# New token layout, order table and engine choices in a two-layer linear-attention and top-2 kernel

## Chip, cores and metric

One core of a Trainium2 chip. The metric is the device time of one execution in microseconds (us). The kernel before takes 153.89 us, the median of 3 runs (153.22 to 154.31).

## What is computed

Two equal layers on x of 2048 tokens by 512, in bfloat16. Each layer is an attention block without a softmax, and then a block that changes two rows only:

```python
q, k, v = layernorm(x) @ wqkv            # 32 heads of 16
phi = lambda t: where(t > 0, t + 1, exp(t)) + 1e-6
kv  = sum over tokens of phi(k)^T v      # per head, no mask
z   = sum over tokens of phi(k)
x   = x + ((phi(q) @ kv) / (phi(q) @ z + 1e-6)) @ wo

h   = layernorm(x)
r   = h @ w_r                            # one number per token
idx = the two tokens with the largest r
y   = (silu(h[idx] @ w_gate) * (h[idx] @ w_up)) @ w_down * sigmoid(r[idx])
x   = x + (h, with y added to rows idx)
```

`w_gate` and `w_up` are 512 by 1376, `w_down` 1376 by 512.

## The kernel before

The 2048 tokens are 16 tiles of 128; tile t holds tokens 128t to 128t+127, one per partition. x (16 tiles by 512 columns), its transpose and all weights stay in SBUF. Loads are cut into blocks of 1, 1, 2, 2, 2, 4 and 4 tiles, and the host arrays A_x and A_xt are laid out block by block so that each partition reads one run.

The kernel is a list of 959 small operations (a layer's products, activations, copies, small statistics). Each names its engine or leaves the choice between VectorE (DVE), ScalarE (ACT) and GpSimd (POOL) open. Two strings settle what is issued when, and where. ORDER (L30 on) names the operations one by one, two characters each, and each engine executes its own in that order; a queue never overtakes. PICK (L64 on) holds one letter for each of the 179 operations with a choice: D, A or P. `Plan.table` (L156) walks through ORDER. Semaphores are set from what each operation reads and writes. PSUM holds 3 slots `mm`, 4 `g` and 1 `tp`, which are reused in ORDER's sequence.

What follows is layer 1 in the order of a reader:

- **Ramp.** TensorE spins on zeros (L862) until the first half of wk lands. Tile 0's raw keys are built from wk and x transposed (L420) and a correction (L426) by wl, the column means of wk, which ScalarE copies from PSUM (L879). VectorE makes wkc, the centred wk, by four additions (L881), and the other tiles' raw keys come from wkc (L420). VectorE's statistics are L338 and L340; the factor 1/sigma is ln and exp on ScalarE (L353, L356), with nb behind it (L361).
- **phi.** For raw keys: e and rl on ScalarE (L393, L394), em on VectorE (L395), and pk = rl + em (L398) on VectorE or POOL. xn, the normalised tile, is L325 (ACT) or L327 (DVE, POOL). G (L438) sums pk^T xn over the tiles; its four matmuls per tile wait for pk and xn.
- **Block mask.** L830 multiplies a head pattern that POOL makes (L773, L775) and leaves a block-diagonal mask, copied at L835 and first read when G becomes KV (L504).
- **Queries.** Q products (L453) and their phi (L375 to L386) fill TensorE; pq is scaled with the denominators at L575, KW = KV times wo is copied from PSUM (L317, L319), and the outputs (L591) are added to x (L596) with sums for the next statistics (L611, L642 to L648).
- **Row choice.** L686 and L689 make keys, one per token, whose low bits hold the token's number (from `rid`, L782). L990 takes each partition's largest, L994 transposes them, L999 takes the candidates. In layer 1 `index(0)` (L1001) turns the two winners into row numbers. In layer 2 the two rows are gathered by matmuls: L1391 broadcasts keys, eqE (L1397) marks candidates, L1451 gathers, WL (L1486), L1497 and L1505 pick, xs (L1514) is the input of gate and up (L1523) and of down (L1564).
- **Last output.** `last_out` normalises a tile of x for the output into pk (L325 or L327), with factors from `last_scales` (L1362 to L1364) and `halves` (L1371, L1372), on any of the three engines. Six stores from SP (L1381) write 4, 4, 2, 2, 2 and 2 tiles; L1581 writes the two chosen rows behind them, with row numbers from L1006 and L1010.

L1435 are matmuls on a zero tile that fill TensorE where it waits.

Of the kernel before, what the change touches and what calls it, by code (L numbers as in the profile page):

```python
# [10 lines left out]
I32 = mybir.dt.int32  # L11
U16 = mybir.dt.uint16
ACT = mybir.ActivationFunctionType
ALU = mybir.AluOpType
# [1645 lines left out]
```

## Time and profile before

| what | us |
|---|---|
| median of 3 runs | 153.89 |
| lowest and highest | 153.22, 154.31 |
| the profiled execution | 154.49 |
| its span, first to last instruction | 152.8 |
| mean granted clock of TensorE | 0.971 |

The rows below come from that one execution. In the profile PE is TensorE, PEld its weight load, DVE VectorE, ACT ScalarE, POOL GpSimd, SP SyncE, and a letter q behind them means the engine's sequencer. Times on the timeline are from the start of the span. A row of the timeline with x4 puts four instructions together, from the first one's start to the last one's end. In brackets stands how long the engine was idle before and what ended that. The granted clock is 1.00 when TensorE may run at its full 2.4 GHz, and 0.5 at 1.2 GHz. Matmuls are pipelined, so one of 0.38 us is followed by the next after 0.215.

### The profile page before, as it was taken

The numbers are of one execution on the slowest core, as the hardware profiler recorded it, in microseconds if no ns is written. First come the engines' busy times: TensorE is split into PE (matmuls) and PEld (weight loads), VectorE is DVE, ScalarE is ACT, GpSimd is POOL, SyncE is SP. The second block draws the span as 40 slices with busy tenths as digits, with TensorE's granted clock in tenths as the row PEclk, the third lists the DMA queues.
The fourth block names the chain that finished last, engine by engine and source line by source line (L and its number), as shares of the span: only waits on it lengthen the run. The fifth ranks groups of instructions, "written<-read, shape, count | busy, mean of one in ns | idle before, by whom it ended". The sixth has DMA issues, their size and how long they took to land.

```text
span 152.8 us, 3668 instructions
## 1 busy us (share of the span) xinstructions
PE 144.9 (95%) x1244; PEld 72.0 (47%) x1262; DVE 125.7 (82%) x456; ACT 111.7 (73%) x270; POOL 43.5 (28%) x101
## 2 busy tenths in 40 slices
PE   7999999999999999999999999999999999995990
PEld 2344444454445544444444454546564445562480
DVE  0599999758889999999999586668889999999550
ACT  3299998697287694998988564335498989999730
POOL 7631522350105433405400003110115056460300
PEclk9999999999999999999999999999999999999685
DMA  5999999569980000489644400000000000004660
GB/s 122 375 356 395 245 312 217 81 122 348 198 330 4 0 4 0 102 180 389 121 75 100 96 12 0 6 0 0 4 0 4 0 0 4 2 0 139 210 206 5
DMA packets 23187, 18.20 MB, mean 119 GB/s; under 512 B 18048, under 2 KB 20608, under 8 KB 22784
## 3 DMA queue, kind: packets, MB, share of 16 engines
q1 hardware_dynamic: 22872, 17.57, 42.8%
q10 hardware_dynamic: 296, 0.39, 0.7%
q8 instruction: 10, 0.16, 0.4%
q14 instruction: 9, 0.07, 0.2%
HBM read 11.67 MB, written 2.10 MB: 90 GB/s over the span
## 4 chain that ended last, share of the span: by engine, by line
PE 79%; DVE 13%; DMA 3%; ACT 2%; issue 1%; DVEq 0%; ACTq 0%
PE g L438 18%; PE mm L453 16%; PE mm L420 9%; PE g L591 9%; PE mm L406 9%; DVE x L596 6%; DMA wk<-in_A_wk_dram 3%; DVE pq L575 2%; PE tp L551 1%; PE g L1435 1%; PE g L492 1%; PE g L1523 1%; PE g L1451 1%; PE mm L1078 1%; PE g L534 1%
## 5 line engine op out<-in xcount | busy, mean ns | idle before, releaser
L375 ACT ACTIVATE e<-mm 128x512 bf16<-128x512 f32 x48 | 28.1, 598 | 10.1 <-PE mm L406 5.6
L453 PE MATMUL mm<-xnT,wq 128*128 128x512 bf16 x119 | 31.2, 380 | 0.5
L438 PE MATMUL g<-pk,xn 128*128 128x512 bf16 x126 | 31.4, 379 | 0.1
L591 PE MATMUL g<-KW,pq 128*128 128x512 bf16 (+2 forms) x128 | 29.8, 373 | 0.2
L611 ACT ACTIVATE sq<-x 128x512 bf16<-128x512 bf16 (+2 forms) x31 | 18.8, 608 | 2.0 <-DVE x L596 1.6
L438 PEld LDWEIGHTS <-xn 128*128 128x128 bf16 x128 | 12.1, 98 | 13.8
L591 PEld LDWEIGHTS <-pq 128*128 128x128 bf16 x132 | 12.2, 97 | 13.1
L453 PEld LDWEIGHTS <-wq 128*128 128x128 bf16 x128 | 11.7, 98 | 13.2 <-issue 0.6
L406 PE MATMUL mm<-wk,xnT 128*128 128x512 bf16 x62 | 16.0, 380 | 0.1
L379 DVE TENSOR_SCALAR em<-e 128x512 bf16<-128x512 bf16 x48 | 13.5, 289 | 3.0 <-ACT e L375 2.7
L420 PE MATMUL mm<-wkc,xt 128*128 128x512 bf16 x59 | 14.3, 379 | 0.1
L338 DVE BATCH_NORM_STATS2 st<-x 128x6 f32<-128x512 bf16 x16 | 10.4, 677 | 4.2 <-DMA x<-in_A_x_dram 4.2
L394 ACT ACTIVATE rl<-mm,rho 128x512 bf16<-128x512 f32 x16 | 11.0, 703 | 1.2 <-issue 1.1
L386 DVE SCALAR_TENSOR_TENSOR pk<-mm,em 128x512 bf16<-128x512 f32 x16 | 11.0, 688 | 0.6 <-DVE em L379 0.4
L393 ACT ACTIVATE e<-mm,rho 128x512 bf16<-128x512 f32 x16 | 10.8, 698 | 0.6 <-PE mm L426 0.6
L596 DVE SCALAR_TENSOR_TENSOR x<-x,opr,g 128x512 bf16<-128x512 bf16 (+2 forms) x17 | 11.3, 710 | 0.0
L386 DVE SCALAR_TENSOR_TENSOR pq<-mm,em 128x512 bf16<-128x512 f32 x16 | 10.7, 686 | 0.2
L596 DVE SCALAR_TENSOR_TENSOR x<-x,g 128x512 bf16<-128x512 bf16 x16 | 10.4, 680 | 0.0
L420 PEld LDWEIGHTS <-xt 128*128 128x128 bf16 x64 | 6.2, 98 | 7.8 <-issue 0.5
L378 ACT ACTIVATE rl<-mm 128x512 bf16<-128x512 f32 x16 | 9.4, 595 | 0.5 <-PE mm L453 0.4
L406 PEld LDWEIGHTS <-xnT 128*128 128x128 bf16 x64 | 6.0, 98 | 7.5 <-issue 0.7
L327 POOL TENSOR_SCALAR xn<-x,s,nb 128x512 bf16<-128x512 bf16 x8 | 6.5, 821 | 10.6 <-DVE nb L361 9.9
(297 smaller groups left out, 243.1 us busy)
## 6 DMA issues: line engine op xcount, KB each, us to landing
wgu<-in_B_wgu_dram SPq DMA_DIRECT2D x2, 1408.0 KB, 6.1
wd<-in_B_wd_dram SPq DMA_DIRECT2D x1, 1408.0 KB, 6.9
xt<-in_A_xt_dram SPq DMA_DIRECT2D x2, 512.0 KB, 6.2
x<-in_A_x_dram SPq DMA_DIRECT2D x2, 512.0 KB, 6.9
out_dram<-pk SPq DMA_DIRECT2D x2, 512.0 KB, 3.1
out_dram<-pk SPq DMA_DIRECT2D x4, 256.0 KB, 2.8
xt<-in_A_xt_dram SPq DMA_DIRECT2D x3, 256.0 KB, 4.2
x<-in_A_x_dram SPq DMA_DIRECT2D x3, 256.0 KB, 4.8
```

Of the source, the lines that this page charges most:

```text
L375: act(0.5, lambda: A.activation(out=e()[:], in_=p()[:], func=ACT.Exp), r=[p], w=[e], **k)
L379: dve(0.2, lambda: V.tensor_scalar(out=em()[:], in0=e()[:], scalar1=1.0, scalar2=TINY, op0=ALU.min, op1=ALU.add), r=[e], w=[em], port=True ...
L386: dve(0.6, lambda: V.scalar_tensor_tensor(out=out_ap, in0=p()[:], scalar=0.0, in1=em()[:], op0=ALU.max, op1=ALU.add), r=[p, em], w=[key], **k)
L393: act(0.57, lambda: A.activation(out=e()[:], in_=p()[:], func=ACT.Exp, scale=s_), r=[p, ("rho0", t)], w=[e])
L394: act(0.57, lambda: A.activation(out=rl()[:], in_=p()[:], func=ACT.Relu, scale=s_), r=[p, ("rho0", t)], w=[rl])
L406: T_.matmul(p()[:], lhsT=xnT[:, c, t * P : (t + 1) * P], rhs=wk[:, c, :], start=(c == 0), stop=(c == NC - 1))
L420: T_.matmul(p()[:], lhsT=xt[:, t, c, :], rhs=w_[:, c, :], start=(c == 0), stop=(c == NC - 1 and not raw))
L438: T_.matmul(Gs[c]()[:], lhsT=xn[:, t, gcol(c) : gcol(c) + P], rhs=pk[:, t, :], start=first, stop=last)
L453: T_.matmul(p()[:], lhsT=wq[:, i, c, :], rhs=xnT[:, i, j * D : (j + 1) * D], start=(i == 0), stop=(i == NC - 1))
L591: T_.matmul(p()[:, 0:n], lhsT=pqt(c, t * P, P), rhs=KWs[layer][:, c, a : a + n], start=(c == 0), stop=(c == NC - 1),)
L596: dve(0.07 + 0.6 * n / D, lambda a=a, n=n, p=p, h=h: V.scalar_tensor_tensor(out=x[:, t, a : a + n], in0=x[:, t, a : a + n], scalar=1.0 if ...
L611: A.activation(out=sq()[:, 0:n], in_=xh, func=ACT.Square, scale=float(D) ** -0.5, accum_out=acc)
```

## The change

Three things change.

First, the token layout: token 16p + t now lies in partition p of tile t. The host arrays, the output's pattern, the numbers in `rid` and `index(0)` follow; `index(0)` has two more small instructions on VectorE. A store of four tiles now writes one run of 4 KB per partition.

Second, ORDER is another sequence of the same 959 operations. In most of it the shifts are local; the larger ones are in the first 30 us and from about 110 us on. On SP's queue the loads keep their order at the start, wd stands right behind the second half of wgu, wvn behind all sixteen transposes of layer 2, and the last three stores are of tiles 14 to 16, 12 to 14, and 10 to 12 instead of 10 to 12, 14 to 16 and 12 to 14.

Third, PICK: VectorE has 77 of the choices (79 before), ScalarE 60 (61), POOL 42 (39). In the ramp pk of tile 0 and xn of tiles 1, 3, 4, 6, 7 and 10 go to POOL; pk of tiles 1, 5 and 8 come to VectorE. In the last quarter one pq addition, one KW copy and a few last_out change engines.

```diff
-    out_dram = out.flatten_outer_dims().rearrange("(t p) d -> p t d", p=P)
+    out_dram = out.flatten_outer_dims().rearrange("(p t) d -> p t d", t=NT)
...
-        G_.iota(rid[:], pattern=[[-P, NT]], base=S - 1, channel_multiplier=-1)
+        G_.iota(rid[:], pattern=[[-1, NT]], base=S - 1, channel_multiplier=-NT)
...
         def f():
-            V.tensor_scalar(
-                out=idx[:], in0=g8[:, 0:2].bitcast(I32), scalar1=S - 1, scalar2=S - 1,
-                op0=ALU.bitwise_and, op1=ALU.bitwise_xor,
-            )
+            bits = g8[:, 0:2].bitcast(I32)
+            if i == 0:
+                V.tensor_scalar(
+                    out=lo_[:], in0=bits, scalar1=7, scalar2=(NT - 1) * P, op0=ALU.logical_shift_left, op1=ALU.bitwise_and
+                )
+                V.tensor_scalar(
+                    out=idx[:], in0=bits, scalar1=4, scalar2=P - 1, op0=ALU.logical_shift_right, op1=ALU.bitwise_and
+                )
+                V.scalar_tensor_tensor(
+                    out=idx[:], in0=lo_[:], scalar=S - 1, in1=idx[:], op0=ALU.bitwise_xor, op1=ALU.bitwise_xor
+                )
+            else:
+                V.tensor_scalar(
+                    out=idx[:], in0=bits, scalar1=S - 1, scalar2=S - 1, op0=ALU.bitwise_and, op1=ALU.bitwise_xor
+                )
...
-        "A_x": blocks(inputs["A_x"].reshape(NT, P, D).transpose(1, 0, 2)),
-        "A_xt": blocks(inputs["A_x"].reshape(NT, P, NC, P).transpose(3, 0, 2, 1)),
+        "A_x": blocks(inputs["A_x"].reshape(P, NT, D)),
+        "A_xt": blocks(inputs["A_x"].reshape(P, NT, NC, P).transpose(3, 1, 2, 0)),
...
 ORDER = (
-    "0P8b000Q01030R020e05060708090A0X0B0k3x040Y450S0W0V0Z0f0T0a0g0U0b0r0l463y0y0m0c0h0i0n0w0C170s0o0t0z0D0E0H0F1D0G0x"
+    "0P000Q03010X0Y040R0S0W3y020506070e08090A0B0C0D0f0Z0V0T0E0U0r0a0g0b0c0k0l0H0F0G0d0i0I0w170h0m0n0j1D0y0o0p0s1C0t0z"
```

The first place is TensorE's start, behind the first four raw-key matmuls (L420) of tile 0. E_94 is the head pattern, wl the correction. This is a piece of the difference:

```order
 L420 LDWEIGHTS xt
 L420 MATMUL mm<-wk,xt 128x512
-L830 LDWEIGHTS E_94
-L830 MATMUL mm<-E_94 128x128
 L426 LDWEIGHTS xt
 L426 MATMUL mm<-wl,xt 128x512
```

L830 has left this place; it stands now behind the products that close layer 1's G.

On POOL, from the last of the constants on, before:

```order
L788 MEMSET elast 128x128
L789 AFFINE_SELECT elast<-elast 128x128
L327 TENSOR_SCALAR xn<-x,rho,nb 128x512
L398 TENSOR_TENSOR pk<-rl,em 128x512
L327 TENSOR_SCALAR xn<-x,rho,nb 128x512
L974 MEMSET h_150 128x352
L398 TENSOR_TENSOR pk<-rl,em 128x512 x2
L327 TENSOR_SCALAR xn<-x,rho,nb 128x512
L398 TENSOR_TENSOR pk<-rl,em 128x512
```

and in the changed kernel:

```order
L788 MEMSET elast 128x128
L789 AFFINE_SELECT elast<-elast 128x128
L327 TENSOR_SCALAR xn<-x,rho,nb 128x512
L398 TENSOR_TENSOR pk<-rl,em 128x512
L327 TENSOR_SCALAR xn<-x,rho,nb 128x512 x3
L819 MEMSET KWr 128x128
L819 MEMSET w_73 128x128
L327 TENSOR_SCALAR xn<-x,rho,nb 128x512 x2
L973 MEMSET eqE 128x384
L327 TENSOR_SCALAR xn<-x,rho,nb 128x512 x2
L820 COPY w_73<-wr 128x4
L398 TENSOR_TENSOR pk<-rl,em 128x512
```

The first pk is now tile 0's (before it was tile 1's), the other pk that follows is tile 10's, and seven xn stand between and behind them.

On VectorE around the largest keys (L990), which L994 on TensorE waits for, before:

```order
L648 TENSOR_TENSOR mv<-mv,sums 128x3
L686 SCALAR_TENSOR_TENSOR s_192<-mv,pwr,s_186 128x1
L990 MAX s_190<-keys 128x8
L1362 TENSOR_SCALAR opr<-rho 128x1
L1363 TENSOR_TENSOR rho<-mv,rho 128x1
L1364 TENSOR_TENSOR nb<-rho 128x1
L686 SCALAR_TENSOR_TENSOR s_189<-mv,pwr,s_186 128x3
L689 TENSOR_TENSOR keys<-s_192,rho 128x1
L999 MAX cand<-tp 128x8
L689 TENSOR_TENSOR keys<-s_189,rho 128x3
L1371 CAST sc<-rho 128x3
L1372 TENSOR_TENSOR sc<-rho,sc 128x3
```

and in the changed kernel, whose lines from L1009 on are 11 higher:

```order
L686 SCALAR_TENSOR_TENSOR s_190<-mv,pwr,s_187 128x3
L689 TENSOR_TENSOR keys<-s_189,rho 128x12
L686 SCALAR_TENSOR_TENSOR s_193<-mv,pwr,s_187 128x1
L648 TENSOR_TENSOR mv<-mv,sums 128x3
L990 MAX s_191<-keys 128x8
L327 TENSOR_SCALAR pk<-x,opr,nb 128x512
L1373 TENSOR_SCALAR opr<-rho 128x1
L1374 TENSOR_TENSOR rho<-mv,rho 128x1
L1375 TENSOR_TENSOR nb<-rho 128x1
L689 TENSOR_TENSOR keys<-s_193,rho 128x1
L999 MAX cand<-tp 128x8
L689 TENSOR_TENSOR keys<-s_190,rho 128x3
```

The key term of the last 3 tiles (L686) stands now ahead of L990, and a final normalisation pk, which stood ahead, right behind it. Further on, three pk stand between WL (L1486, now L1497) and xs (L1514, now L1525) on VectorE, where one pair stood behind xs before.

## Rows read from the trace of the kernel before

**Rows 1.** The page's first part: busy time, share of the span, instructions

```profile
PE 144.9 (95%) x1244; PEld 72.0 (47%) x1262; DVE 125.7 (82%) x456; ACT 111.7 (73%) x270; POOL 43.5 (28%) x101
```

**Rows 2.** Waits of PE, whole span: us, times, longest

```profile
PE tp L994 <- DVE rho L1363: 1.6, 1, 1.6
```

**Rows 3.** Busy time by stretches: PE, PEld, DVE, ACT, POOL, PEclk, DMA share, GB/s

```profile
134.00:138.00 4.00, 3.83 (x48) 2.16 (x46) 3.97 (x23) 3.92 (x17) 2.62 (x8) 1.00 0.06 22
138.00:142.00 4.00, 2.43 (x20) 1.26 (x24) 3.58 (x26) 3.92 (x8) 0.60 (x4) 0.83 0.46 155
142.00:146.00 4.00, 4.00 (x83) 2.35 (x76) 2.20 (x10) 3.11 (x4) 0.91 (x2) 0.74 0.59 197
```

**Rows 4.** Timeline 137.5 to 146.5: start, duration, engine, line, operation, idle before

```profile
139.21 0.16 DVE L990 MAX8 s<-keys 128x8 f32<-128x12 f32 x1
...
139.52 0.40 PE L994 MATMUL tp<-identf,s 128*128 128x128 f32 x2 [1.64 <-DVE rho L1363]
...
139.96 0.43 DVE L999 MAX8 cand<-tp 128x8 f32<-128x256 f32 x1
...
140.31 0.15 DVE L689 TENSOR_TENSOR keys<-s,rho 128x3 bf16<-128x3 f32 x1
...
142.75 1.45 PE L1435 MATMUL g<-warm 128*128 128x512 bf16 x3
...
143.21 0.51 DVE L1486 SCALAR_TENSOR_TENSOR WL<-keys,s,sc 128x45 bf16<-128x45 f32 x2
...
144.84 0.17 DVE L1514 TENSOR_REDUCE xs<-tp 128x8 bf16<-128x16 f32 x1 [1.12 <-PE tp L1505]
```

**Rows 5.** The chain that ended last, in time: start, time on the chain, engine, line

```profile
135.89 2.00 DVE x L596 x6
...
140.52 0.82 PE mm L1391 x3
...
145.25 1.78 PE g L1523 x72
...
147.61 1.19 PE g L1564 x44
```

**Rows 6.** Timeline 146.4 to the end, the row number and the row write

```profile
147.75 0.16 DVE L1010 SCALAR_TENSOR_TENSOR s<-s 128x1 int32<-128x1 int32 x1
...
149.57 1.14 ACTq L1581 DMA_DIRECT2D out_dram<-yo  x1
```

**Rows 7.** Timeline of the ramp, 0 to 13.5

```profile
5.38 1.29 DVE L338 BATCH_NORM_STATS2 st<-x 128x6 f32<-128x512 bf16 x2 [4.22 <-DMA x<-in_A_x_dram]
...
5.83 0.60 ACT L879 ACTIVATE wl<-g 128x512 bf16<-128x512 f32 x1 [2.79 <-PE g L876]
...
6.59 0.23 PE L830 MATMUL mm<-E 8*128 8x128 bf16 x1
6.66 1.40 DVE L881 TENSOR_TENSOR wkc<-wk,wl 128x512 bf16<-128x512 bf16 x4
...
6.75 1.04 PE L426 MATMUL mm<-wl,xt 128*128 128x512 bf16 x4
...
7.88 0.69 ACT L393 ACTIVATE e<-mm,rho 128x512 bf16<-128x512 f32 x1 [0.57 <-PE mm L426]
...
10.48 1.03 PE L438 MATMUL g<-pk,xn 128*128 128x512 bf16 x4
```

**Rows 8.** Line 398 (pk): durations in ns min/median/max, first and last start

```profile
L398 DVE TENSOR_TENSOR pk<-rl,em x12: 384/419/426, 9.9 to 35.8; 128x512 bf16<-128x512 bf16 x12
L398 POOL TENSOR_TENSOR pk<-rl,em x4: 1148/1153/1157, 11.0 to 28.1; 128x512 bf16<-128x512 bf16 x4
```

**Rows 9.** DVE's groups by form: count | busy us, mean ns | idle before

```profile
L596 DVE SCALAR_TENSOR_TENSOR x<-x,opr,g 128x512 bf16<-128x512 bf16 x15 | 10.5, 741 | 0.0
...
L327 DVE TENSOR_SCALAR pk<-x,opr,nb 128x512 bf16<-128x512 bf16 x4 | 1.5, 406 | 0.0
...
L686 DVE SCALAR_TENSOR_TENSOR s<-mv,pwr,s 128x3 f32<-128x3 f32 x1 | 0.2, 216 | 0.0
```

More of the change, by code (lines that the diff above doesn't have):

```diff
@@ new lines @@
+    "271r2D1u1g1s0L1S2A1v3z341h1i3E1w1j2R2Z2E2G252Q2F2H2I2J353F2j2u2v26362B1x2C2U2e372w2a202x3j4C1y2K382b8Z2k2L2M2f3G"
+    "4D211z1k3H302c2d2S2T2z393I3J2g3l3k2l2N2h401Q3A2y3U2i312m320M3x2O2n333B3C3D3P2o3Q2p2s4E3m8a3n3S2q2r3Z3b3a3e3K3L3R"
+    "3c3d3T3p3r3q4J4K4L4M442V4F3o3s3N2W2X2t3O4G4H4I3V3u3v3t3w3W4O4N3M3X3Y2Y47485349544A4Q4P4R4S55564r4s8c3f3g454d4e46"
+    "4t4u3h3i4f4T4U4z50514g4h4j4v4w4x524y4k4V4X0N4i4l4m4Z4W4a4b4c5V4Y5W4n4o4q4p5O0O57585X5P5L5S5Q5R595A5B5M5N5T5U5E5F"
+    "5G5D5Z5a5Y5b6P5o6Q5p5c5C5d5q5e5r5s5t5u5H5I5v6B5J6I5K5n5w5x5y626R6y64655f685g6C6D60618X5h66635i6z696A6r6J6X75765j"
@@ new lines @@
+    "6S7C5k8b67706K6E6W5m5l7n8I6Y6T6s6Z6a6b6c7D6d7u6t6F6e6f6U6V777E6g6G6H6h6n6lA3A5A46j8J7oALAM6k7K414BAN7L8P8Q7v7M7N"
+    "6pA9AA6o6L6MABAC7O7P7QAO6N6O7p7J7R7S7T7UAP6u6v81827a6w6x9r7W7wAF7172736m7c839wAD6qAGAH7bA17d84858K74787X79Aj7qAl"
+    "8eAkA27FA87V8R7A8fAI7Y8g868788898AAJ7B7Z8B8C8G8H8EAE427r7s7G7e7H8h8i7I8j7f7g8F8k8l7h8m7i9f9g7t8d8n8o8s8t8q9h7x7y"
+    "8p7z8LAK7j805z6i43AQ7k7l7m8D8r8M8u8N8xAX8v8OAm8w8y8S8T8z9192AYAZ9iAn93949DAWAc96Ad999sAe8U989A8VAiAf9B9C979E9FAo"
+    "9M9G9t9J9u9vAz9NA695909KB09H9IAR9L9P9O9Q9R9jAa9k9l9m9n9o9SA7Ag9UAx9T9p9xAS8WAT9y9q9V9W9XApAqAr9zA09Y9ZAt9a9cB49b"
@@ new lines @@
+    "AUAbB1B28YAVAs9eBLBN9dBMBFBGBHBvAuAvBxBwAhC7BKAwBqBIB8BOBQAyC8CAB9ByC9CBBrBtBsBABPBBBJCTBcBRB3BdBeB6BzBYB5B7BjBk"
+    "BuBUBWBSBCBDBlBZBaBbBfBVBgCZBECbCaBmBnBXCCCECDC0C1BTC2CKCLBhBiCWClCcBoBpCdCMC3C4CFCXCmCnCYCGCHCNCOCICJC5CoCpCqDI"
+    "DJCeCfCgCsCtCuCvC6DFDCDGDKD3DHCrDDCwCyChCiCPCSCQCRDED4CUDMDLCVCkCjD5DND1CxD0DODPDQDVDRDmDnDoDgDjDhDkDXDYDiDlDpEQ"
+    "D6DZD8ERD7D9EUESETEVDqElDAEmDrEnDsDBEDEoEpEECzD2DtDwDxEGEHE4E5DaDbDdDcDeE7EAE8EJEqEKE9EBDfECDuEODvErEWEFEIE6ELEX"
+    "DSEwEYEsEaDTEtEZEMENEPEhEiEjDyEbDUDWEcEdEuExF1EkF2EgEvEeF3DzE2EfEzF0FDFFEyFEE1F4F5F6F7E0E3FGF8FCFHFIF9FAFNFJFKFL"
@@ L49 @@
+    "FOFMFBFQFPFRFS"
 )
@@ L1001, in index @@
     def index(i):
-        idx, pw = small([P, 2], I32), small([P, 1], I32)
+        idx, pw, lo_ = small([P, 2], I32), small([P, 1], I32), small([P, 2], I32)
         g8 = B["g8"]
         def f():
-            V.tensor_scalar(
-                out=idx[:], in0=g8[:, 0:2].bitcast(I32), scalar1=S - 1, scalar2=S - 1,
-                op0=ALU.bitwise_and, op1=ALU.bitwise_xor,
-            )
+            bits = g8[:, 0:2].bitcast(I32)
[13 more added lines that the diff above has]
+                )
             V.scalar_tensor_tensor(
@@ L1012, in f @@
             )
-        dve(0.25, f, r=["g8"], w=["pw"], port=True)
+        dve(0.25 if i else 0.5, f, r=["g8"], w=["pw"], port=True)
         B["idx"], B["pw"] = idx, pw
```

22 lines of the change are left out of this document (3 added, 19 removed).

## The prediction, made before the changed kernel ran

> **What bounds the kernel now.** I began with the shares of the engines: TensorE is busy 144.9 us, 95% of the span, VectorE 125.7 [rows 1]. Next come the waits of TensorE over the whole span: apart from its start there is one, 1.6 us in front of L994, the transposes of the top keys [rows 2]. So up to 137.9 us, where that wait begins (139.52 less 1.64 [rows 4]), nothing that the kernel reorders can be worth more than the little that TensorE loses in steps too short for that list. Third, the stretches of 4 us show who rules the end: VectorE is busy 3.97 us of 4 in 134–138; then TensorE falls to 2.43 us in 138–142, and its granted clock to 0.83 there and 0.74 in 142–146 [rows 3]. With two levels, 1.2 and 2.4 GHz (0.5 and 1), these are 1.4 us of the first and 2.1 us of the second stretch at the lower one, so about 140.6 to 144.1 if they are one piece. The reader is to see three regimes: a ramp in which each TensorE wait counts in full; a long middle with no slack on TensorE; and, from about 117 us, VectorE's queue, which sets when the keys of the last row choice are ready and so when L994 may start. Behind L994 stands a serial tail: L994 139.52, the candidates L999 139.96, the late keys L689 140.31, their broadcasts L1391 140.52, the gather L1451, filling matmuls 142.75, the weights WL 143.21, the sums xs 144.84, gate and up L1523 145.25, down L1564 147.61, and the row writes 149.57 [rows 4 to 6].
>
> The profiled execution is 154.49 us, 0.60 above the median of 153.89; every time below is a difference in that execution, and I carry the sum over to the median unchanged.
>
> **The ramp.** Two things leave the place between the loads and the first G. The block-mask matmul L830 stood between the halves of the first raw-key product: it ran 6.59 to 6.82, and the second half started at 6.75 although its operand wl was done at 6.43 [rows 7]. Behind it, VectorE had two statistics in a row, 5.38 to 6.67, and only then the four additions L881, 6.66 to 8.06, for which the next raw-key products wait [rows 7]. In the new order one statistic stands ahead of the additions and the second behind, so the additions wait for wl: 6.43 plus the step of some 0.1 that other hand-overs take, 6.52. That is 0.14 earlier; the second half may start about 0.16 earlier. I take 0.15. The other end is 0, and the reason is pk(0). Its addition goes from VectorE to POOL, where four additions of that line took 1.153 against 0.419 on VectorE [rows 8]. ScalarE now does e(0) and rl(0) in one row, without the small lnv between them, so with the second half at 6.6 e(0) would start at 7.72 (1.13 behind it, as 7.88 behind 6.75) and both, at 0.69 each, be done at about 9.0 to 9.1; POOL ends at about 10.2, and G(0) wants pk at 10.48 − 0.15 = 10.33 [rows 7]. It fits with a tenth to spare. If it does not, the gain of the ramp is gone first, and what POOL is later than 10.33 is paid one for one.
>
> The trace's ratio of these additions is 2.75. The Trainium skill, in "GPSIMD Engine Reference", § 4.1 Engine selection, sends elementwise work to VectorE and puts two-input operations on GpSimd at about twice as slow. By that ratio the addition would take an estimated 0.84, pk(0) would be ready at 9.9 and no wait would be possible; by the row there is one tenth. The measurement decides.
>
> The xn of tiles 1, 3, 4, 6, 7 and 10 that go to POOL will be slower there too, up to the 0.73 of the addition as a bound, but each is wanted by a G with at least one raw-key product of four matmuls (1.03 [rows 7]) between; pk(1), (5) and (8) come back to VectorE in exchange. I put this at nothing, with those products as cover.
>
> **The layout.** Loads keep their size, their order and one run per partition, because the host array is permuted with them: 0. Stores write one run of 4 KB per partition where they wrote four of 1 KB. The row writes, which wait for all stores, left at 149.57 [rows 6]. But they wait for the row number too: L1010 ends at 147.91 [rows 6], and the registers are loaded behind it. That path is the same in both kernels, so faster stores gain nothing that can be relied on: 0, with 0.2 as the other end. The two additional small instructions of the first row choice (0.16 each, as L1010 [rows 6]) lie beside TensorE's filling work in layer 1: 0. The wvn load moves behind all transposes of the second layer; its first reader, L1239, stands far behind them, where layer 2 turns from keys to outputs: 0.
>
> **VectorE in the last quarter.** Between the first scaling of pq (L575) and the keys' maximum L990 the new order takes out two means (0.16 each, as other small instructions of VectorE [rows 6]) and one final normalisation pk (0.406), and takes in one key term of 3 columns (L686, 0.216) [rows 9]: −0.51 busy. Between KVm (L504) and that first scaling it moves one small instruction (0.16, L677) ahead and puts one pq addition of 0.42 (as L398 [rows 8]) in: +0.26. One KW copy takes the place of another. From KVm on the sum is thus −0.25. A busy microsecond is less than one of the clock, because records overlap: three of the residual additions L596, 0.741 each, and the three short reads of their accumulators (the x6 of the row) carry the chain on by only 2.00, where the additions alone are 2.22 [rows 5, 9]. With the reads I count five sixths. So L990 comes 0.21 to 0.43 earlier, by whether the additional pq addition lies in time that VectorE spent waiting for TensorE's KV products or not. I take 0.30, nearer the low end, since VectorE's queue was already full ahead of the first scaling.
>
> **What is given back behind L990.** The pk that was taken out stands now right behind L990, ahead of the three small scale instructions, the last-but-one key and L999. In before L999 started 0.75 after L990, as soon as L994's result was there (139.52 + 0.40) [rows 4]. Now VectorE has 0.41 more and the 0.22 of L686 less in front of it: L990 + 0.95. The late keys L689 follow L999 by 0.35 as before, and their broadcasts L1391 started 0.2 after 140.31 [rows 4, 5]. So +0.20. The two half-precision instructions that leave the place before eqE make eqE about 0.3 earlier, but L1451 has to wait for L1391 (140.52 + 0.82) anyway: 0.
>
> **The tail.** t15's final normalisation leaves ScalarE, so the table load for the gate starts earlier; but the gate and up products fill TensorE without a break until 147.4 (145.25 + 1.78 and the rest) [rows 5]: 0. Three pk on VectorE now stand between WL (ends 143.72) and xs (144.84) [rows 4]. Three times 0.406 [rows 9] is 1.22 busy, about 1.0 to 1.1 of the clock, in a hole of 1.12: 0, with +0.1 as the near end and one pk, +0.4, as the far end.
>
> **The sum.** −0.15 − 0.30 + 0.20 = −0.25. The profiled execution would be 154.24, the median **153.64**, rounded 153.6. The bounds of the terms together give −0.8 (−0.16, −0.43, 0, −0.2) to +0.6 (0, −0.21, +0.2, +0.4, and 0.2 of waiting for pk(0)).
>
> **Rivals.** *The clock stays up.* TensorE's granted clock is halved from about 140.6 to 144.1 [rows 3], behind the wait of 1.64 us. Three filling matmuls then took 1.45, while four of the same width took 1.03 at the full level [rows 4, 7]; three would take 0.8, so 0.65 is lost there, and the gather between 141.3 and 142.75, all at the lower level, could give some 0.5 more, of which VectorE's WL takes a part back. The new order shortens the wait by about 0.3. If that is enough to keep the full level, the tail gains a further 0.8: 152.8. Against it: the wait is still 1.3 us, and the waits for the late keys and for eqE remain. The opposite phase, with the half level over L1523, costs little: 72 matmuls there took 1.78, 24.7 ns each, and 44 of L1564, later, 1.19, 27 ns each [rows 5].
>
> The Trainium skill says in "TensorE: Matmul & The Clock Gate", Part 1, that the clock follows TensorE's recent activity and has two levels; by that rule a shorter wait would bring the 152.8 of this rival; the granted clock, which falls only behind the wait, agrees so far [rows 3].
>
> *Slower.* POOL's additions set the ramp: TensorE has no gap there in which to hide a late pk. The place is G(0), the point from which it decides is rl(0) later than 9.2 (10.33 − 1.15), and each POOL addition that is on the path instead of VectorE's costs 0.73 [rows 8]. One such gives 153.64 + 0.15 + 0.73 = 154.5; a second one, at G(1) or by way of a PSUM bank that frees late, 155.2. For it: the spare is a tenth. Against it: only pk(0) and pk(10) stand on POOL in the ramp, where before it was pk(1), (5), (8) and (10).
>
> *It does nothing at the end.* VectorE's queue is full from another cause, L990 comes 0.2 earlier, and the pk behind it gives that back: only the ramp is left, or not even that: 153.8 to 153.9.
>
> **How the numbers follow.** Forecast 0.50 (153.2 to 154.0); nothing 0.17 (153.7 to 154.2); clock 0.15 (152.8); slower 0.18 (154.5 to 155.6). The range leaves out the upper part of the slower case and the lower edge of the clock's: 152.6 to 154.8. About 1%, 1.5 us, is what a measurement of this kernel can tell from no change: below 152.35 only the clock case with every bound at its good end, 0.10; above 155.43 the slower case with two late additions, 0.10; within, 0.80.
>
> **What would show it.** Right: the second half of the raw-key product at about 6.6 and the additions L881 at 6.5; G(0) at 10.3 with no wait of TensorE for POOL; L990 near 138.75 and L999 about 0.95 behind it; TensorE's wait at L994 near 1.3; xs right behind its matmuls; the spans of the tail as before. Wrong: a wait of TensorE for POOL's pk in 10 to 12 us, xs late behind pk, or a granted clock near 1 in 141 to 144.

## The result, and the profile of the changed kernel

The changed kernel takes **154.80 us** (median of 6 runs, 154.66 to 155.03), the kernel before 153.88 on the same chip (153.22 to 154.31). The ratio is 1.0061 with an interval of 1.0036 to 1.0087: 0.9 us slower, by less than 1%. The forecast was 153.6, 0.25 faster; the time lies on the upper edge of the range. The profiled execution of the changed kernel took 154.73, its span is 153.0. Executions over 1.5% slower than the fastest of their kernel (one of late_plus2, two of the kernel before) count in no number below.

The shares say little. This is the page's first part, the answer to [rows 1]; VectorE is 3.4 us busier, TensorE is not:

```profile
PE 144.7 (95%) x1243; PEld 72.5 (47%) x1262; DVE 129.1 (84%) x456; ACT 111.7 (73%) x269; POOL 44.8 (29%) x104
```

The waits of TensorE over the whole span (us, times, longest), the answer to [rows 2], show two things: the wait in front of L994 has become longer instead of shorter, and there is a new one, in front of a query product (L453).

```profile
PE tp L994 <- DVE s L990: 1.9, 1, 1.9
...
PE mm L453 <- ACT e L393: 0.3, 1, 0.3
```

The stretches of 4 us (busy time of PE, PEld, DVE, ACT, POOL, then the granted clock, DMA share and GB/s) answer [rows 3]. VectorE, which had been busy 3.97 of 4 us in 134–138, is busy 3.59: it stands still there. The granted clock falls, as in the profiled execution of before.

```profile
134.00:138.00 4.00, 3.95 (x56) 2.44 (x54) 3.59 (x19) 3.61 (x16) 2.53 (x8) 1.00 0.01 2
138.00:142.00 4.00, 2.02 (x13) 1.08 (x16) 3.90 (x29) 3.96 (x11) 0.58 (x4) 0.90 0.33 133
142.00:146.00 4.00, 4.00 (x68) 1.96 (x64) 2.99 (x12) 3.18 (x4) 1.24 (x5) 0.68 0.51 201
```

The timeline of the end (start, duration, engine, line, operation, idle before), the answer to [rows 4], has L990 at 139.75 where 138.75 was forecast, and L994 0.54 later than before:

```profile
139.75 0.17 DVE L990 MAX8 s<-keys 128x8 f32<-128x12 f32 x1
...
140.06 0.40 PE L994 MATMUL tp<-identf,s 128*128 128x128 f32 x2 [1.91 <-DVE s L990]
...
140.54 0.43 DVE L999 MAX8 cand<-tp 128x8 f32<-128x256 f32 x1
...
143.34 1.42 PE L1446 MATMUL g<-warm 128*128 128x512 bf16 x3
...
145.41 0.17 DVE L1525 TENSOR_REDUCE xs<-tp 128x8 bf16<-128x16 f32 x1
```

The step in which the lateness begins is a small one. VectorE's timeline in the last quarter:

```profile
135.88 0.15 DVE L681 TENSOR_TENSOR s<-s,s 128x4 f32<-128x4 f32 x1
136.45 0.16 DVE L626 SCALAR_TENSOR_TENSOR s<-s2x,mv 128x1 f32<-128x1 f32 x1 [0.41 <-ACT lnv L353]
136.52 0.74 DVE L596 SCALAR_TENSOR_TENSOR x<-x,opr,g 128x512 bf16<-128x512 bf16 x1
```

L626, one column, is 0.41 us late, and the trace puts this down to an instruction of ScalarE (lnv) that L626 doesn't read. What the program makes L626 wait for was done: ScalarE's square of the first 320 columns (L611) by 135.86, VectorE's L624 by 135.97. Nothing in the prediction spoke of it.

The ramp went as forecast up to the first G. Its timeline answers [rows 7]: the additions L881 at 6.52, the second raw-key half (L426) at 6.55, the POOL addition of pk(0) from 9.19 to 10.34, G(0) right behind it with no wait for POOL.

```profile
5.69 1.03 PE L420 MATMUL mm<-wk,xt 128*128 128x512 bf16 x4
...
6.52 1.43 DVE L881 TENSOR_TENSOR wkc<-wk,wl 128x512 bf16<-128x512 bf16 x4
6.55 1.03 PE L426 MATMUL mm<-wl,xt 128*128 128x512 bf16 x4
...
9.19 1.15 POOL L398 TENSOR_TENSOR pk<-rl,em 128x512 bf16<-128x512 bf16 x1 [0.29 <-ACT lnv L353]
...
10.39 0.81 PE L438 MATMUL g<-pk,xn 128*128 128x512 bf16 x3
```

### The profile page after: what moved, and what is told of

It is laid out like the page before. It is cut to its first block, busy times and chain, and to the rows that moved or that the text cites. A ratio compares the mean times of both kernels' runs of the same rounds, so it can differ in the third digit from the quotient of the medians.

```text
span 153.0 us, 3655 instructions
## 1 busy us (share of the span) xinstructions
PE 144.7 (95%) x1243; PEld 72.5 (47%) x1262; DVE 129.1 (84%) x456; ACT 111.7 (73%) x269; POOL 44.8 (29%) x104
## 4 chain that ended last, share of the span: by engine, by line
PE 70%; DVE 18%; ACT 6%; issue 3%; DVEq 0%; ACTq 0%
PE g L438 17%; PE mm L453 14%; PE g L591 9%; PE mm L406 8%; PE mm L420 7%; DVE x L596 5%; DVE pq L575 3%; ACT sq L611 3%; PE tp L862 3%; DVE em L379 2%; ACT e L375 1%; PE g L1446 1%; PE g L1534 1%; PE mm L1089 1%; PE g L1462 1%
## 5 line engine op out<-in xcount | busy, mean ns | idle before, releaser
L453 PE MATMUL mm<-xnT,wq 128*128 128x512 bf16 x121 | 31.0, 379 | 0.7 <-ACT e L393 0.3
L438 PE MATMUL g<-pk,xn 128*128 128x512 bf16 x125 | 30.7, 379 | 0.3 <-issue 0.2
L591 PE MATMUL g<-KW,pq 128*128 128x512 bf16 (+2 forms) x127 | 29.2, 373 | 0.2
L611 ACT ACTIVATE sq<-x 128x512 bf16<-128x512 bf16 (+2 forms) x31 | 18.9, 610 | 1.0 <-DVE x L596 0.6
L453 PEld LDWEIGHTS <-wq 128*128 128x128 bf16 x128 | 11.8, 97 | 13.6 <-issue 1.5
L379 DVE TENSOR_SCALAR em<-e 128x512 bf16<-128x512 bf16 x48 | 14.6, 310 | 2.1 <-ACT e L375 0.9
L406 PE MATMUL mm<-wk,xnT 128*128 128x512 bf16 x62 | 15.5, 379 | 0.1
L420 PE MATMUL mm<-wkc,xt 128*128 128x512 bf16 x58 | 14.1, 379 | 0.1
L383 POOL TENSOR_TENSOR pq<-rl,em 128x512 bf16<-128x512 bf16 x6 | 7.2, 1202 | 20.4 <-DVE em L379 9.4
L575 POOL TENSOR_TENSOR pq<-pq,rd 128x1024 bf16<-128x1024 bf16 x3 | 6.3, 2097 | 18.8 <-DVE em L379 14.4
L386 DVE SCALAR_TENSOR_TENSOR pk<-mm,em 128x512 bf16<-128x512 f32 x16 | 11.0, 688 | 0.3
L386 DVE SCALAR_TENSOR_TENSOR pq<-mm,em 128x512 bf16<-128x512 f32 x16 | 10.9, 689 | 0.4
L420 PEld LDWEIGHTS <-xt 128*128 128x128 bf16 x64 | 6.2, 98 | 7.9 <-issue 0.6
```

The costliest lines, as they stand in the source:

```text
L379: dve(0.2, lambda: V.tensor_scalar(out=em()[:], in0=e()[:], scalar1=1.0, scalar2=TINY, op0=ALU.min, op1=ALU.add), r=[e], w=[em], port=True ...
L386: dve(0.6, lambda: V.scalar_tensor_tensor(out=out_ap, in0=p()[:], scalar=0.0, in1=em()[:], op0=ALU.max, op1=ALU.add), r=[p, em], w=[key], **k)
L406: T_.matmul(p()[:], lhsT=xnT[:, c, t * P : (t + 1) * P], rhs=wk[:, c, :], start=(c == 0), stop=(c == NC - 1))
L420: T_.matmul(p()[:], lhsT=xt[:, t, c, :], rhs=w_[:, c, :], start=(c == 0), stop=(c == NC - 1 and not raw))
L438: T_.matmul(Gs[c]()[:], lhsT=xn[:, t, gcol(c) : gcol(c) + P], rhs=pk[:, t, :], start=first, stop=last)
L453: T_.matmul(p()[:], lhsT=wq[:, i, c, :], rhs=xnT[:, i, j * D : (j + 1) * D], start=(i == 0), stop=(i == NC - 1))
```

## The experiments

Ratios are to runs of the kernel before on the same chip; medians of two kernels that ran on different chips are best compared by them. "Operations 1 to k" counts in the order table; a kernel that takes one table up to k and the other behind it takes the engine choices with them. The last two columns are TensorE's wait at the merge of the top keys (L994, from the list of waits) and the share of executions whose mean granted clock was 0.976 or less (in the others it was 0.978 to 0.991).

| kernel | layout | order | us | ratio, interval | wait | low clock |
|---|---|---|---|---|---|---|
| changed kernel | new | new | 154.80 | 1.0061 [1.0036, 1.0087] | 1.9 | 6 of 6 |
| layout_only | new | old | 153.93 | 0.9980 [0.9952, 1.0007] | 1.6 | 2 of 10 |
| order_only | old | new | 154.77 | 1.0044 [1.0016, 1.0072] | 1.5 | 3 of 10 |
| ramp_new | old | new to 280 | 155.01 | 1.0054 [1.0030, 1.0078] | 1.6 | 7 of 10 |
| quarter_new | old | new 681 to 855 | 156.34 | 1.0121 [1.0070, 1.0171] | 1.8 | 4 of 4 |
| wv_later | new | new, one moved | 154.80 | 1.0061 [1.0036, 1.0086] | 1.9 | 4 of 5 |
| rest_new | new | old to 280, new | 153.74 | 0.9986 [0.9960, 1.0012] | 1.5 | 2 of 10 |
| end_new | new | old to 855, new | 153.57 | 0.9973 [0.9950, 0.9997] | 1.4 | 1 of 10 |
| ramp_wv | new | new to 280, one moved | 154.76 | 1.0054 [1.0038, 1.0071] | 1.6 | 2 of 7 |
| after_hot6 | new | new | 155.44 | 1.0082 [1.0051, 1.0114] | 0.8 | 0 of 6 |
| end_hot6 | new | as end_new | 154.35 | 1.0018 [0.9993, 1.0042] | 0.3 | 0 of 12 |
| early_new | new | new to the first G | 155.40 | 1.0074 [1.0049, 1.0098] | 1.7 | 5 of 6 |
| late_new | new | old to the first G, new | 153.76 | 0.9974 [0.9957, 0.9991] | 1.5 | 1 of 12 |
| late_stall | new | as late_new | 154.19 | 1.0001 [0.9980, 1.0022] | 1.9 | 4 of 11 |
| late_plus2 | new | as late_new | 154.45 | 1.0014 [0.9987, 1.0041] | 1.9 | 4 of 10 |
| after_plus10 | new | new | 154.25 | 0.9987 [0.9960, 1.0014] | 1.5 | 4 of 11 |
| after_again | new | new | 155.01 | 1.0058 [1.0037, 1.0079] | 1.9 | 9 of 11 |
| after_plus2 | new | new | 154.32 | 1.0013 [0.9987, 1.0039] | 1.5 | 1 of 11 |
| after_plus4 | new | new | 154.26 | 1.0015 [0.9993, 1.0038] | 1.5 | 1 of 11 |

### Which part of the change: layout, ramp or last quarter

**layout_only**

```diff
 out_dram, rid, index(0), host arrays: as in the changed kernel
-ORDER, PICK: the new tables
+ORDER, PICK: the old tables
```

> New token layout, old ORDER and PICK. Theory A: within 0.2 us of before; the stores land sooner, which the row write may not see. Theory B: 154.6 to 155.0. Theory C (the layout gives back what the order costs): 153.3 to 153.6, because the end waits for the last store.

153.93 against 154.22 for before on that chip: 0.3 less, with an interval that just takes in no change. What follows: the layout doesn't cost; it may give a little.

**order_only**

```diff
-out_dram = out.flatten_outer_dims().rearrange("(p t) d -> p t d", t=NT)
+out_dram = out.flatten_outer_dims().rearrange("(t p) d -> p t d", p=P)
 (and rid, index(0), host arrays as before; ORDER, PICK: the new tables)
```

> Old token layout, new ORDER and PICK. Theory A (the order costs it): in the trace after, TensorE loses 0.43 us once at 36 us and VectorE 0.4 us once at 136 us, both set by the order, so nearly all of the +0.9 us is here: 154.6 to 155.0, L990 near 139.75. Theory B (the layout costs it): within 0.2 us of the kernel before, 153.7 to 154.1.

154.77, 0.55 more than before on that chip. The new order costs, the layout doesn't. In its profile L626 follows L681 without a wait, and TensorE waits 1.5 at the merge, 0.1 less than before.

**ramp_new** and **quarter_new**, both with the old layout:

```diff
 ramp_new
-ORDER: operations 1 to 280 of the old table
+ORDER: operations 1 to 280 of the new table (to about 45 us), the old behind them
 quarter_new
-ORDER: operations 681 to 855 as in the old table
+ORDER: operations 681 to 855 as in the new table (about 108 to 135 us)
```

> Old layout; new ORDER and PICK for the first 280 operations (to about 45 us), old behind them. Theory A: G(0) 0.1 us earlier, then one wait of TensorE of 0.4 us near 36 us, so the last quarter and the end are 0.2 to 0.35 us later: 154.1 to 154.3. Theory D (lateness of TensorE in the ramp is swallowed later, because VectorE rules the last quarter): 153.9.

> Old layout; old ORDER and PICK except for the operations 680 to 854 (about 108 to 135.5 us), which stand in the new order and on the new engines. Theory A: the first scaling of pq 0.1 to 0.3 us later, L990 0.2 to 0.5 us later by the wait of L626 for ScalarE, 154.1 to 154.4. The prediction's own reading (less work on VectorE) gives L990 0.2 to 0.4 earlier, 153.5.

The ramp's new order alone costs 0.8 us. quarter_new costs 1.9 by the ratio, but 1.0 of it is a wait that the joint makes (TensorE's L453 waits for POOL's xn transposed, L1273, at 110.33), so it says nothing clear of the changed kernel.

### Is it the wait for a PSUM buffer at 36 us?

**wv_later**: the centring of wv, 1.21 us of VectorE, stands ahead of a pk in the new order; the pk frees the buffer for ScalarE's rl of raw key 15, and ScalarE's e behind that frees the PSUM buffer for which L453 waits.

```diff
-    ...2s4E3m8a3n3S...3c3d3T3p3r...
+    ...2s3m8a3n3S...3c3d3T4E3p3r...
```

> The changed kernel (154.80 us) with one operation of its table moved: the centring of wv on VectorE (1.21 us) stands behind the product of raw key 12 instead of ahead of the product of raw key 14. Theory A (the order's loss begins in the ramp): the product of raw key 14 ends at about 33.5 instead of 34.68, so ScalarE's relu of raw key 15 no longer waits for its buffer, its exponential ends near 35.4, the PSUM buffer is free when the Q product of tile n6 wants it, TensorE's gap of 0.27 us before it goes, and by far the most of that comes through: 154.80 - 0.25 to 0.45 = 154.35 to 154.55. Theory D (lateness in the ramp is swallowed by waits further on, the loss sits in the last quarter): the gap goes and the time stays 154.7 to 154.9, with VectorE's second-order difference of the last quarter at 139.7 as before.

154.80, as without the move. The wait of 0.27 is gone, but the next query product then waits 0.16, and TensorE is only 0.1 earlier at 45 us.

**ramp_wv** is the same move with the new order up to operation 280 only, **rest_new** the opposite, **end_new** only what lies behind operation 855.

```diff
 rest_new
-ORDER: operations 1 to 280 of the new table
+ORDER: operations 1 to 280 of the old table, the new behind them
 end_new
+ORDER: operations 1 to 855 of the old table, the new behind them
 ramp_wv
+ORDER: operations 1 to 280 of the new table, 4E behind 3T; the old behind them
```

> The new layout, the old order up to operation 280 (about 45 us), the new order behind it. Theory A (the ramp's order costs 0.8 us, the rest nothing): 153.9 to 154.0, that of the new layout with the old order, 0.8 to 0.9 below the changed kernel. Theory D (the last quarter's order costs it): 154.6 to 154.9, and the second-order difference of the keys on VectorE as late against the filling matmuls' end as in the changed kernel.

> The new layout, the old order up to operation 855 (about 135.4 us), the new order behind it: the key projections on ScalarE and POOL instead of VectorE, the second-order difference moved ahead, three products of keys ahead of the last states. Against the new layout with the old order (153.93 us). The prediction's own reading: 0.1 to 0.3 lower, 153.6 to 153.85. Theory C (the loss sits in this stretch, by way of what ScalarE and POOL give VectorE too late): 154.2 to 154.8.

> The new layout, the new order up to operation 280 with the centring of wv moved as in wv_later, the old order behind it. If the ramp's loss of 0.8 us (old layout) is that one wait, 153.9 to 154.1, and 153.8 if the ramp's gain of 0.15 at the first G matmul then shows too. If the ramp's order costs more than that wait, 154.4 to 154.8.

With the old ramp the new order costs nothing: 153.74 and 153.57. With the new ramp it is 154.76 even without that wait. So the loss starts in the ramp, but the wait at 36 us is not its main part.

### Which part of the ramp

**late_new** and **early_new** cut at the first G matmul, at about 10 us.

```diff
 late_new
-ORDER: operations 1 to 63 of the new table
+ORDER: operations 1 to 63 of the old table, the new behind them
 early_new
+ORDER: operations 1 to 54 of the new table; masks (POOL) and L830 as late as in the
+new table (behind pk(10), behind the products of wot); the rest of the old table
```

> The changed kernel with the old order up to the first G matmul (63 operations), and with that POOL's masks and L830 in the ramp's pause again. Theory R by its parts: TensorE saves L830's 0.2 us but not the wait of 0.27 us at 36 us, so 154.5 to 154.7. Theory E (all of the ramp's loss comes out of its first 12 us): 153.7 to 153.9, as with the whole old ramp (153.74). Theory M (none of it does): 154.8.

> The new layout and, of the new order, only what leads to the first G matmul (its first 54 operations), with POOL's masks (3.6 us) and the small transpose of L830 behind it at about 25 and 34 us; the rest of the order is old. Compared with the new layout and the old order, 153.93 us. The prediction's term for the ramp: -0.15, and L830's 0.2 us comes back in the full stream of TensorE: 153.9 to 154.0. If the work on POOL in the ramp delays what follows it: 154.3 to 154.8.

late_new is 1.04 us faster than the changed kernel (1.3 by the ratios) and differs from it in 12 us. early_new is 1.5 us slower than layout_only by the ratios; it has three waits of TensorE of its own (0.22, 0.35 and 0.16 us at 13.5, 35.4 and 35.8), so only its sign counts.

In the trace the cost is seen on TensorE. The same product (L551) in the changed kernel and in late_new, then the first G of late_new:

```profile
44.56 0.23 PE L830 MATMUL mm<-E 8*128 8x128 bf16 x1
44.71 0.41 PE L551 MATMUL tp<-pq,Z 128*32 128x128 bf16 x16
```

```profile
6.25 1.03 PE L420 MATMUL mm<-wk,xt 128*128 128x512 bf16 x4
7.21 0.23 PE L830 MATMUL mm<-E 8*128 8x128 bf16 x1
...
11.09 1.03 PE L438 MATMUL g<-pk,xn 128*128 128x512 bf16 x4
...
44.83 0.41 PE L551 MATMUL tp<-pq,Z 128*32 128x128 bf16 x16
```

From the first raw-key matmul to G(0) the changed kernel needs 4.70 us, late_new 4.84: the forecast 0.15. (In the profiled executions with the old order this stretch took from 4.7 us, in rest_new and late_plus2, to 5.2, in layout_only, so one pair of executions doesn't measure the gain.) From G(0) to L551 the changed kernel needs 34.32, late_new 33.74: 0.58 more. Together 0.44 lost. L830 is 0.15 of the 0.58 (44.56 to 44.71); it stood in a pause of the ramp and stands now in a stream without pauses. The rest is the new wait in front of L453:

```profile
33.94 1.89 PE L453 MATMUL mm<-xnT,wq 128*128 128x512 bf16 x8
...
36.09 1.02 PE L453 MATMUL mm<-xnT,wq 128*128 128x512 bf16 x3 [0.27 <-ACT e L393]
```

Eight matmuls from 33.94 on, one after 0.215 us, make the next due at 35.66; it starts 0.43 later. (The trace counts 0.27 as idle, because the record of a matmul is longer than its step.) late_new has no such wait, because VectorE is 0.5 earlier there. What made it late, as the trace shows it, is POOL's masks, moved out of the pause for the loads together with L830; no run moved the masks alone. VectorE's rows and POOL's in the changed kernel, and the same two of VectorE in late_new:

```profile
31.45 0.61 DVE L361 SCALAR_TENSOR_TENSOR nb<-mv,rho 128x2 f32<-128x2 f32 x1
32.09 0.80 DVE L327 TENSOR_SCALAR xn<-x,rho,nb 128x512 bf16<-128x512 bf16 x1
```

```profile
30.81 0.52 POOL L773 MEMSET E<- 128x512 bf16 x1
31.40 1.34 POOL L775 TENSOR_SCALAR_AFFINE_SELECT E<-E 128x512 bf16<-128x512 bf16 x2
```

```profile
32.49 0.15 DVE L361 SCALAR_TENSOR_TENSOR nb<-mv,rho 128x2 f32<-128x2 f32 x1
32.68 0.41 DVE L327 TENSOR_SCALAR xn<-x,rho,nb 128x512 bf16<-128x512 bf16 x1
```

Beside the masks two VectorE instructions take 0.46 and 0.39 longer. The Trainium skill, in "Advanced Engine Details and Errata", section VectorE Performance Modes, says that VectorE's second port to SBUF is shared with GpSimd, and that GpSimd's instructions and those of VectorE that use two ports block each other. The two rows agree, but no run shows which ports an instruction uses.

### Does the clock decide?

The wait at L994 is 1.9 us, and the granted clock falls behind it. **after_hot6** and **end_hot6** put five more free matmuls into it.

```diff
-    hot(1, [("lt", NJ - 1, NJ - 1), "Odone"], "hot1")
+    hot(6, [("lt", NJ - 1, NJ - 1), "Odone"], "hot1")
```

> The changed kernel with six instead of one of the free matmuls that stand ahead of the merge of the first candidates (call of hot before topk, L1457 in the numbering of the changed kernel): 5 x 0.2155 = 1.08 us of matmuls in a wait of 1.91 us. Theory K (that wait decides whether TensorE's clock falls behind it; in the profiled executions it was 1.8 to 1.9 us where the granted clock fell at once, 1.6 where it fell in part of them, 1.4 to 1.5 where it stayed): the granted clock stays 1.00 from 138 to 146 in the profile, the last stretch is 0.9 to 1.1 us shorter than the changed kernel's, mean clocks are 0.98 to 0.99, and the time is 154.80 - 0.9 = 153.8 to 154.1. Theory R (the loss is TensorE's work and waits of the ramp, the clock has its own ways): 154.7 to 154.9, mean clocks 0.972 to 0.975.

> The new layout, the old order up to operation 855, the new order behind it (153.57 us), with the same five more free matmuls in a wait of 1.4 us. Theory K: nearly all of its executions kept the clock there already (one of ten had a mean of 0.972), so 153.4 to 153.6. Theory R: 153.5 to 153.7, no difference. If the matmuls are in the way of the merge: later by what of 1.08 us the wait does not cover, up to 153.9.

The mean clock stayed at 0.98 to 0.99 in all 18 executions, and yet neither kernel is faster: by the ratios end_hot6 is 0.7 us slower than end_new, and after_hot6 0.3 slower than the changed kernel, which is not clear of noise. The span of after_hot6 is shorter than the changed kernel's (152.65 against 153.1 in the median) and that of end_hot6 like end_new's (151.7, 151.55), but the time outside the span grew from 1.7 to 2.0 to a median of 2.75 and 2.6. I didn't find out why; as a remedy it failed.

### The wait before L626

Three kernels that ran by then had the 0.41 us before L626 (the changed kernel, wv_later, after_hot6), all with the new layout and the same first twelve microseconds and end; order_only, rest_new and late_new have the same instructions around L626 and no such wait. What differs is the place of L626 in VectorE's list of instructions (counted in the program, its waits included): 416 in those three, from 414 to 427 in all others, but not 416. It is the two instructions added to `index(0)` that bring it there: order_only, without them, has it at 414. late_plus2 and the three after_plus kernels test the place, late_stall puts real work where the wait was.

**late_stall**

```diff
-        tiny([lambda: V.scalar_tensor_tensor(
+        late_ = big.tile([P, D], BF16, name="late_")
+        tiny([lambda: (V.tensor_single_scalar(out=late_[:], in_=wl[:], scalar=1.0, op=ALU.mult), V.scalar_tensor_tensor(
             out=b[:], in0=s2x[:, 1, 0:1], scalar=EPS, in1=v, op0=ALU.add, op1=ALU.add
```

**late_plus2** (late_new with n = 2), **after_plus10**, **after_plus4**, **after_plus2** (the changed kernel with n = 10, 4, 2) and **after_again** (the changed kernel):

```diff
     nc.vector.memset(nmean[:], -1.0 / D)
+    pad = big.tile([P, n], BF16, name="pad")
+    for i in range(n):
+        nc.vector.memset(pad[:, i : i + 1], 0.0)
```

> late_new (153.76 us) with one more VectorE instruction, a copy of 128x512 into a spare tile (about 0.41 us by the row of such an operation), ahead of L626 in the last quarter; the copy is read by nobody. Theory K (TensorE's wait ahead of the merge, 1.54 us there and 1.9 then, decides how often the clock falls): 153.76 + 0.4 + 0.3 to 0.6 = 154.4 to 154.8, with mean clocks of 0.971 to 0.976 in most executions. Theory L (the lateness itself, no more): 154.1 to 154.2. Theory S (swallowed): 153.7 to 153.9.

> late_new with two more VectorE instructions at the program's start, memsets of one column each, where VectorE waits for the loads. L626 is then as far down VectorE's list as in the changed kernel (instruction 416 instead of 414). Theory F (the wait of 0.41 us before L626 depends on where in VectorE's list it stands): the wait appears, TensorE waits 1.9 us at the merge, and the time is that of late_stall. Otherwise: no wait there, 153.7 to 153.9.

> The changed kernel with ten such memsets of one column at the start, L626 is instruction 426 instead of 416. Theory F: the wait of 0.41 us before L626 is gone, TensorE waits 1.5 us at the merge, and of the changed kernel's 154.80 us what the TensorE stream of the ramp costs is left over the 153.76 us of late_new: 154.1 to 154.4. Otherwise: 154.7 to 154.9 with the wait.

> The changed kernel once more, on the same chip as the three others: 154.7 to 154.9, mean clocks of 0.972 to 0.975, the wait of 0.41 us before L626 (Theory F: it belongs to the program and not to the execution).

> The changed kernel with two VectorE memsets of one column at the start; L626 is instruction 418 of VectorE's list. Theory F: no wait of 0.41 us before L626 (it belongs to place 416), TensorE waits 1.5 us at the merge, 154.1 to 154.4 as with ten memsets. If the wait goes to the instruction that stands at place 416 now, the time stays 154.7 to 155.0 with the wait somewhere in the short instructions ahead of L626.

> The same with four memsets; L626 is instruction 420. Theory F: 154.1 to 154.4, no wait at L626. If the wait goes with place 416: 154.7 to 155.0, and a wait of about 0.4 us earlier among the short instructions.

The wait comes and goes with the place. VectorE's timeline of late_new, of late_plus2 (lines 3 higher) and of after_plus2:

```profile
136.06 0.16 DVE L681 TENSOR_TENSOR s<-s,s 128x4 f32<-128x4 f32 x1
136.24 0.16 DVE L626 SCALAR_TENSOR_TENSOR s<-s2x,mv 128x1 f32<-128x1 f32 x1
```

```profile
136.44 0.15 DVE L684 TENSOR_TENSOR s<-s,s 128x4 f32<-128x4 f32 x1
137.00 0.16 DVE L629 SCALAR_TENSOR_TENSOR s<-s2x,mv 128x1 f32<-128x1 f32 x1 [0.41 <-ACT lnv L356]
```

```profile
136.09 0.15 DVE L684 TENSOR_TENSOR s<-s,s 128x4 f32<-128x4 f32 x1
136.28 0.16 DVE L629 SCALAR_TENSOR_TENSOR s<-s2x,mv 128x1 f32<-128x1 f32 x1
```

It takes L626 at that place, though, and not the place alone: what stands at 416 in after_plus2 (L684 at 136.09), after_plus4, after_plus10 and late_new starts right behind its predecessor.

The waits of TensorE of late_plus2, then of after_plus2, go along, while the wait of the ramp stays where the ramp's order is the new one:

```profile
PE tp L997 <- DVE s L993: 1.9, 1, 1.9
```

```profile
PE tp L997 <- DVE s L993: 1.5, 1, 1.5
...
PE mm L456 <- ACT e L396: 0.3, 1, 0.3
```

Two memsets of one column, in a pause, cost late_new 0.7 us (153.76 to 154.45; 0.6 by the ratios); two, four or ten of them make the changed kernel 0.5 us faster (0.76 in the one group that holds after_again too, 155.01 against 154.25). late_stall lies between: its copy makes L990 0.36 later against TensorE's last filling matmul, TensorE's wait 1.9 us again, and the kernel 0.4 us slower, no more. A real lateness at that place is paid once. With the wait, low mean clocks are more frequent (23 of 32 executions in the changed kernel twice, wv_later and late_plus2; 7 of 45 in late_new and the three after_plus kernels), so that part of the 0.5 to 0.8 beyond 0.4 may be the clock. That is not shown: the three executions of the changed kernel and wv_later with a higher clock took 154.80, 155.11 and 155.13 us, no less than the others. late_stall, with the same 1.9 us at the merge, had a low clock in 4 of 11; so the length of the wait alone doesn't set it.

## Why the prediction was wrong, point by point

Two steps failed above all. Work that was moved (L830 and POOL's masks) was priced at nothing where it goes, and it cost TensorE's stream 0.58 us. And an instruction was taken to cost the same at another place of VectorE's list, where L626 came 0.41 us late.

The ratios chain into one sum, each step from one kernel to the next: the layout takes 0.2% (layout_only); the new order behind the first G 0.06% more (late_new), not to be told from nothing; the new order ahead of it adds 0.31% (the three after_plus kernels, 1.0005 in the mean); the wait before L626 adds 0.56%. In us, at 154: −0.31 − 0.09 + 0.48 + 0.86 = +0.94, and 0.92 was measured. The sum closes by construction, since each kernel is compared with its neighbour in the chain; only the steps say something. Each step's interval is about ±0.4 us; the 0.48 has its own witness in the trace, 0.44.

**The ramp, −0.15: right up to G(0), wrong as a term.** The steps came at the forecast places, pk(0) was ready with a twentieth to spare, and TensorE didn't wait for POOL. The step that failed is the one that took L830 out of its place at no price. What the ramp gained up to G(0), 0.14, L830 takes back where nothing waits, 0.15. POOL's masks were not priced at all: they were free beside the loads, and beside VectorE they stretched two of its instructions by 0.85, made it 0.5 late and TensorE, through a PSUM buffer, 0.43. Measured +0.44 instead of −0.15. The slower rival named a PSUM bank that frees late, but by way of POOL's additions; its place and its price were others.

**The layout, 0: low by 0.3, by a step that failed.** I took the path from the row number to the row writes for the same in both kernels. Its instructions are the same, but one of them became shorter: the load of the row number into registers (TENSOR_LOAD, L1027, now L1038). From the end of L1010 to the first row write it is 1.66 us in the kernel before (147.91, 149.57), and 1.34 in layout_only (148.04, 149.38) and in the changed kernel (148.47, 149.81). The four waits of SP for the stores (EVENT_SEMAPHORE, with their first and last start) pass one after the other in the kernel before and in layout_only, so the row writes waited there for the row number and not for a store, as forecast. In order_only they don't:

```profile
L1027 SPq TENSOR_LOAD <-s x1: 766/766/766, 147.9 to 147.9; - x1
L1581 SPq EVENT_SEMAPHORE  x4: 17/28/28, 149.3 to 149.4; - x4
```

```profile
L1038 SPq TENSOR_LOAD <-s x1: 482/482/482, 148.1 to 148.1; - x1
L1592 SPq EVENT_SEMAPHORE  x4: 17/28/28, 149.1 to 149.3; - x4
```

```profile
L1581 SPq EVENT_SEMAPHORE  x4: 17/28/28, 148.7 to 149.5; - x4
```

The load takes 0.76 to 0.80 us in the four profiles with the old layout, and with the new one 0.48 in 13 of 16 (0.56, 0.72 and 0.75 in the others). Why, no run shows. The stores are on their way then, and the larger ones land sooner, after 2.6 or 2.7 us in all profiles with the new layout and 3.0 or 3.1 with the old (KB each, us to landing; first the changed kernel, then the kernel before):

```profile
out_dram<-pk SPq DMA_DIRECT2D x2, 512.0 KB, 2.7
```

```profile
out_dram<-pk SPq DMA_DIRECT2D x2, 512.0 KB, 3.1
```

The last store sets the row writes only where the tail is earlier: order_only has its row number early (L1010 at 147.22) and yo done at 148.80, and yet the row writes leave at 149.67. In rest_new, too, they leave 0.7 behind yo. The size, 0.3, has an interval that reaches zero.

**VectorE in the last quarter, −0.30, and the give-back, +0.20: both too large, their sum nearly right.** Without the wait before L626, TensorE waits 1.54 us at the merge with the new order (order_only, rest_new and late_new alike; late_new's row is shown) where it was 1.64 [rows 4]: 0.1, not 0.3.

```profile
139.87 0.40 PE L994 MATMUL tp<-identf,s 128*128 128x128 f32 x2 [1.54 <-DVE s L990]
```

From L646 to L990 VectorE needs 4.07 us in late_new (135.48 to 139.55) and 4.26 before (134.95 to 139.21): 0.19 less, and half of that is lost again ahead of L646. L999 follows L990 by 0.79 in the changed kernel where it was 0.75 [rows 4]: 0.04 given back, not 0.20. That the two misses cancel, −0.06 where −0.10 was forecast, is luck.

**The tail, 0: right.** xs starts at 145.41, 0.04 behind the end of its matmuls; three pk ahead of it were no hindrance.

**What no step held.** The largest single part is what goes with the 0.41 us before L626. No list of busy times and no view of the kernel before could have given it, since L626 stood there at another place of the list; it belongs into the range, not into the sum. The forecast counted as if the same instruction at another place took the same time. The clock's rival failed too: the clock stayed up where TensorE was kept busy, and the kernel was not faster for it. Where it stays up by itself the rival's 0.8 is about right: of the kernel before's executions beside the experiments, the 36 with a mean clock above 0.983 have a median of 153.71 us, the 40 with 0.976 or less 154.42. And the granted clock falls not only behind the wait: in both profiled executions it is 0.50 in 148–150 too, behind two microseconds in which TensorE was busy 2.00 of 2.

**What stays open.** Why L626 is late at place 416, and other instructions at that place are not; what the rest of the 0.86 is; why matmuls in the wait lengthen the time outside the span; why the register load is shorter with the new layout; and 0.6 us in ramp_wv, which by the ratios is 1.1 slower than layout_only, of which TensorE's stream behind G(0) shows 0.5.

end_new and late_new are faster than both kernels, by 0.27% and 0.26% against before, with intervals that stay below 1.

## What to carry to other kernels

Price a moved instruction twice: what it frees where it stood, and what it costs where it goes. Out of a pause into a full stream it costs what it delays the next one by, and a POOL instruction set beside VectorE can cost VectorE too. Before a change of order of half a per cent is blamed or praised, run it once more with two or four empty instructions at the start: if the time moves, a part of it belongs to the place in the list and not to the order.

## What the runs showed of the hardware

The place of an instruction in VectorE's list can cost time: 0.41 us before instruction 416 in all five profiled executions that had L626 there, none before L626 at 414, 418, 420 or 426 with the same neighbours, none before what stood at 416 in late_new and the three after_plus kernels, and 0.6 us of the kernel's time (by the ratios) moved by two memsets of one column. The trace names a releaser that L626 doesn't read.

POOL's memsets and selects can stretch VectorE's instructions beside them: 0.15 to 0.61 us for two columns, 0.41 to 0.80 for 512. Not all: the L386 just ahead of these two, at 30.84, took its usual 0.69 beside the same masks.

The load of one number from SBUF into SP's registers took 0.76 to 0.78 us with the old layout's stores on their way, and 0.48 in most profiles with the new layout's.

The level of TensorE's clock in the last 15 us differs between executions of one kernel (mean 0.970 to 0.991 for the kernel before), and in the kernel before the time went with it by 0.7 us, so that medians of four to twelve executions, not the profiled one, had to carry every comparison here.
